# Linear-attention layer: the product of kv and wo from rounded halves, and who scales two of the queries

## The chip, the cores and the metric

The kernel runs on one core of one Trainium2 chip. The metric is the device time of one execution in microseconds (us). Three runs of the kernel before gave 863.69, 865.16 and 864.30 us, median 864.3 us.

A core has five instruction streams that run side by side: TensorE (PE, matrix products; its weight loads are listed as PEld), VectorE (DVE), ScalarE (ACT), GpSimd (POOL) and SyncE (SP), which here only starts DMA transfers. Each stream executes strictly in its program order and waits on semaphores for the others.

## The reference

Two layers, each an attention block A and an MLP block B, all in float32 on x of 2048 tokens by 448 features:

```
x = x + A(layernorm(x));  x = x + B(layernorm(x))        (twice)
A: q, k, v = split(x @ wqkv) in 16 heads of 28
   pq, pk = phi(q), phi(k),  phi(t) = (t + 1 if t > 0 else exp(t)) + 1e-6
   kv  = sum over tokens of pk^T v          (28 x 28 for each head)
   z   = sum over tokens of pk
   den = pq . z + 1e-6
   out = concat over heads(pq @ kv / den) @ wo
B: gelu(x @ w1 + b1) @ w2 + b2
```

## The kernel before

**Rounded halves.** TensorE multiplies plain float32 slowly, and a rounded format, `fp32r`, quickly. Most products are therefore made from two halves, a high half (a copy rounded to fp32r) and a low half (the original minus the high half): high times high, high times low and low times high are accumulated in one PSUM bank. A few small products are done in plain float32 instead, kv (`trans_kv`) and M (`trans_m`) among them.

**Phase 1** goes over the 16 token tiles of 128 (`phase1`, steps in `STEPS`). In each step it makes k of a tile, phi(k), its halves `kh` and `kl`, the running sum `za`, and the product G = (normalised x)^T phi(k) of the tile before. Queries phi(q) go to DRAM (`pq_d`). The last step of phase 1 in each layer is step 15.

**Between the halves of the layer** stands the passage that the change rewrites. Its order is written out by hand as a string of tokens, `ORDER`, the same for both layers; each token emits the instructions of one small function, and each engine executes its instructions in that order. The steps are: `G` (the last tile's G, with z), `gt` (G out of PSUM into four tiles), `kv` (kvp = gt^T times the v weights, 448x448 of which only the heads' blocks count), `mask` (DVE: kvm = kvp times a block mask), `m0` to `m3` (`trans_m`: M's row groups mp = kvm^T wo, 112 rows by 448 columns each, plain float32, into the four banks tagged `acc`), and `ms0` to `ms3` (`trans_ms`: Mh by ACT, Ml by DVE). With M = blockdiag(kv) @ wo the attention output is one product of scaled queries with M.

Meanwhile the first four query tiles are prepared: `qz` (POOL: pz = pq times z), `dz` (ACT: a small constant), `qd` (DVE: sum dn per head, then its reciprocal rd), `qt` (DVE: pq times rd; `qs` is `qd` and `qt` together), `tq` (PE: transpose into PSUM), `qh` (ACT: high half), `ql` (DVE: low half), and `o` (PE: twelve fp32r matmuls op, into a bank tagged `acc`). The four op banks are the same four banks that mp used: the first op, that of query 1, takes the bank of m0's result and can start only after `Ml` of that group has read it. Between these stand projections that were put off (`Q`, and `Qx`, `Qu`, `Qy` for a projection in three pieces) and `Qp`, a phi of such a projection (ACT, POOL).

After the four op blocks, five projections keep TensorE busy while the normalised rows are turned and redistributed through DRAM; then the MLP starts (hp, line 1006) and goes over blocks of 512 tokens, preparing the queries of the next block behind the matmuls.

**Tiles** of 448 columns tagged `H` hold rows of x (nine buffers in rotation), `W0` to `W6` hold the halves of the k weights in phase 1 and queries and kvm later, `S` (five buffers) stages weights, `E` and `F` (two each) hold halves. The wo rows arrive on the SP queue (`trans_load`) in two transfers after step 13.

Of the kernel before, what the change touches and what calls it, by code (L numbers as in the profile page):

```python
# [22 lines left out]
def linear_attn_mlp_kernel(  # L23
# [41 lines left out]
    NH = 9  # L65

    def t448(tag, bufs, name, dt=F32):
        bufs = NH if tag == "H" else bufs
        return work.tile([128, D], dt, name=name, tag=tag, bufs=bufs)

    APART = 28
# [7 lines left out]


    xt = {}

    def load_x(l, t):
        xt[l, t] = t448("H", 8, f"x{l}_{t}")
        sp.dma_start(xt[l, t], x_d[l][t * 128:(t + 1) * 128, :])

    load_x(0, 0)
# [550 lines left out]
    def stage_g(l, t, acc, mid=lambda: None):  # L638
# [20 lines left out]


    ORDER = [
# [3 lines left out]
    ] * LAYERS  # L665
    DEFER = NT - sum(tok in ("Q", "Qa", "Qy") for tok in ORDER[0].split())
# [15 lines left out]
    }  # L682
    NORM = (
        ((2,), (3,), (5, 6), (7, 8), (9,), (10,), (11,), (12,), (13,), (14,), (15,)),
# [42 lines left out]
    def phase1(l, tr):  # L727
        za = consts.tile([128, D], F32, name="za", tag="za")
        acc = []
        load_to(l, 4 if l == 0 else NORM[l][1][-1])  # L730
        if l == 0:
            launch(za)
            load_to(l, NORM[l][2][-1])
        for t in range(l == 0, NT):
            norm = NORM[l][t] if t < len(NORM[l]) else ()
            for tok in STEPS.get((l, t), STEP).split():
                if tok[1:].isdigit() and tok[0] in "anv":
                    {"a": stage_a, "n": stage_n, "v": stage_t}[tok[0]](l, int(tok[1:]))
                elif tok == "q1":
                    stage_qphi(1)  # L740
                elif tok == "sp":
                    for key, h in list(stored):
                        block(key)
                        spread(key, h)
                elif tok == "ld" and t + 2 < len(NORM[l]):
                    load_to(l, NORM[l][t + 2][-1])
                elif tok == "a":
                    for u in norm:
                        stage_a(l, u)
                elif tok == "n":  # L750
                    for u in norm:
                        stage_n(l, u)
                elif tok == "tu":
                    for u in norm:
                        stage_t(l, u)
                elif tok == "T" and t + 1 < NT:
                    stage_b(l, t + 1, "acc" if t == 1 else "h")
                elif tok == "X" and t + 1 < NT and (l == 0 or t + 1 >= 4):
                    stage_x(l, t + 1)
                elif tok == "K":  # L760
                    stage_k(l, t)
                elif tok == "qp":
                    stage_qphi()
                elif tok == "kp":
                    stage_kphi(l, t)
                elif tok == "kh":
                    stage_kh(l, t)
                elif tok == "kl":
                    stage_kl(l, t, za)
                elif tok == "s":  # L770
                    stage_s(l, t)
                elif tok == "G" and t >= 1:
                    acc = acc or [bank("acc", 4, f"G{c}")[:, :D] for c in range(4)]
                    stage_g(l, t - 1, acc)
                elif tok == "bg" and l == 0:
                    background(BG[t], 1 if t >= 8 else 2)
                elif tok == "Q" and t < DEFER:
                    stage_q(l, t)
            if t == 12:
                tr.wv = stage_square(wqkv[:, 2 * D:])  # L780
            if t == 13:
                trans_load(l, tr)
        return za, acc


    def trans_load(l, tr):
        tr.wo = []
        for h in range(2):
            s = half("wot")[:G, :2 * D].rearrange("p (g n) -> p g n", g=2)
            sp.dma_start(s, wo[h * 2 * G:(h + 1) * 2 * G, :].rearrange("(g p) n -> p g n", p=G))  # L790
            tr.wo += [s[:, 0], s[:, 1]]

    def trans_z(tr, za):
        zp = bank("m", 2, "zp")[:, :D]
# [8 lines left out]
    def trans_gt(tr, acc):  # L803
        tr.gt = []
        for c in range(4):
            s = t512("A" if c < 2 else "B", 2, "gt")[:, :D]
            if c < 3:
                act.copy(s, acc[c])
            else:
                dve.tensor_copy(s, acc[c])  # L810
            tr.gt.append(s)

    def trans_kv(tr):
# [6 lines left out]
    def trans_mask(tr):  # L820
# [2 lines left out]
                          tr.kvp.rearrange("p (g d) -> p g d", g=NG),  # L823
                          mask[:, None, :].to_broadcast([G, NG, G]), op=OP.mult)

    def trans_m(tr, g):
        mp = bank("acc", 4, "mp")[:G, :D]
        pe.matmul(mp, tr.kvm[:, g * G:(g + 1) * G], tr.wo[g], start=True, stop=True)  # L828
        tr.mp[g] = mp

    def trans_ms(tr, g):
        if g == 0:
# [63 lines left out]
    def q_times(l, b, j):  # L896
        pq = pqt[l, b * 4 + j]
        p3 = pq.rearrange("p (h d) -> p h d", d=DH)
        dve.scalar_tensor_tensor(p3, p3, 1e-6, rds.pop((l, b, j))[:, :, None].to_broadcast([128, H, DH]),
                                 op0=OP.add, op1=OP.mult)  # L900

    def q_scale(l, b, j, tr):
        q_den(l, b, j, tr)
# [251 lines left out]
    for l in range(LAYERS):  # L1155
# [11 lines left out]
        def pre(j):  # L1167
# [8 lines left out]
            Qx=lambda j: stage_q(l, fill[0], (0, 1)), Qu=lambda j: stage_q(l, fill[0], (2,)), Qy=lambda j: stage_q(l, fill.pop(0), (3,)),  # L1176
            Qa=lambda j: stage_q(l, fill.pop(0), tag="acc"), G=lambda j: stage_g(l, NT - 1, acc, lambda: trans_z(tr, zs[l])),
            ld=lambda j: (load_pq(l, 0, j), load_x(l, j)), gt=lambda j: trans_gt(tr, acc),
            kv=lambda j: trans_kv(tr), mask=lambda j: trans_mask(tr), m=lambda j: trans_m(tr, j),
            ms=lambda j: trans_ms(tr, j), qz=lambda j: q_z(l, 0, j, tr), qs=lambda j: q_scale(l, 0, j, tr),  # L1180
            dz=lambda j: times_tiny(pzs[l, 0, j][:, :, DH], tr.dc), dc=lambda j: times_tiny(tr.dc, tr.dc),
            qd=lambda j: q_den(l, 0, j, tr), qt=lambda j: q_times(l, 0, j),
# [75 lines left out]
```

## Time and profile before

| what | value |
|---|---|
| median of three runs | 864.3 us |
| the profiled execution: its own time, its span | 864.28 us, 862.6 us |
| PE busy | 857.9 us, 99% |
| DVE, ACT, POOL busy | 57%, 41%, 24% |
| granted TensorE clock | 1.0 throughout |
| the passage between the halves, from the end of kv to the first op | 107.03 to 112.30 us in layer 0, 531.64 to 536.90 us in layer 1 |
| the M product (mp, line 828) | 16 records for 8 products: each float32 product shows as two |

How to read it: an "x32" in a row is a count of records. Rows of the timeline give the start in us, the duration, engine, line and operands, and in brackets how long the engine idled before it and what released it. A matmul's recorded duration overlaps that of the next one, so what it costs TensorE is the distance from its start to the next start.

### The profile page before, as it was taken

To read this page: it belongs to the slowest core of one execution; us is meant where nothing else is said; L and a number is where in the kernel's file an instruction comes from. 1 tells how busy PE (TensorE), PEld (TensorE's weight loads), DVE (VectorE), ACT (ScalarE), POOL (GpSimd) and SP (SyncE) were. 2 spreads that over 40 slices of the span, in tenths; PEclk is the share of its full clock that TensorE was granted. 3 is DMA by queue.
4 is the path that set the end of the run, shared out by engine and by line. 5 is a ranking of instruction groups with operands and counts; after the bars stand their busy time and mean duration, and the time that the engine had idled before them with its cause. 6 is when DMAs were issued, how large, how long until landed. Compare 5 with 4: busy or idle time off the path is not lost.

```text
span 862.6 us, 11717 instructions
## 1 busy us (share of the span) xinstructions
PE 857.9 (99%) x4155; PEld 768.7 (89%) x4155; DVE 492.4 (57%) x962; ACT 353.0 (41%) x635; POOL 210.4 (24%) x244
## 2 busy tenths in 40 slices
PE   9999999999999999999999999999999999999998
PEld 8999988888888888888899998988888888888887
DVE  7888586559456443236477876764664383533112
ACT  7676655323323322333356565633232233233231
POOL 3576612235013012012222343120310140140000
PEclk9999999999999999999999999999999999999999
DMA  5485647633313402051145443462332423111001
GB/s 171 148 283 171 205 112 217 189 113 126 118 66 122 137 0 98 1 182 49 49 152 188 163 130 97 150 200 81 124 115 76 140 74 111 49 49 43 1 1 43
DMA packets 68681, 97.89 MB, mean 113 GB/s; under 512 B 9488, under 2 KB 62864, under 8 KB 68624
## 3 DMA queue, kind: packets, MB, share of 16 engines
q1 hardware_dynamic: 67872, 96.76, 34.8%
q8 instruction: 32, 0.52, 0.3%
q10 hardware_dynamic: 752, 0.41, 0.2%
q14 instruction: 25, 0.20, 0.1%
HBM read 57.74 MB, written 36.18 MB: 109 GB/s over the span
## 4 chain that ended last, share of the span: by engine, by line
PE 99%; DVE 0%; issue 0%; DVEq 0%
PE hp L1006 32%; PE y L1036 10%; PE y L1035 10%; PE y L1037 10%; PE G L652 8%; PE psk L366 8%; PE psq L366 7%; PE op L943 2%; PE op L942 2%; PE op L944 2%; PE op L932 1%; PE op L931 1%; PE op L933 1%; PE kvp L818 1%; PE mp L828 1%; PE psk L580 1%
## 5 line engine op out<-in xcount | busy, mean ns | idle before, releaser
L1012 DVE TENSOR_TENSOR gl<-g,gh 128x512 fp32r<-128x512 f32 x112 | 83.2, 743 | 292.8 <-ACT gh L1011 292.8
L1008 ACT ACTIVATE g<-hp,b1s 128x512 f32<-128x512 f32 x112 | 77.0, 688 | 400.9 <-PE hp L1006 400.9
L1036 PE MATMUL y<-w2l,gh 128*128 128x448 f32 x447 | 163.6, 366 | 0.0
L1035 PE MATMUL y<-w2h,gh 128*128 128x448 f32 x447 | 162.0, 362 | 0.0
L1037 PE MATMUL y<-w2h,gl 128*128 128x448 f32 x447 | 160.1, 358 | 0.0
L1006 PE MATMUL hp<-XH,w1l 128*128 128x512 f32 x336 | 130.7, 389 | 0.0
L1006 PE MATMUL hp<-XH,w1h 128*128 128x512 f32 x336 | 130.7, 389 | 0.0
L1006 PE MATMUL hp<-XL,w1h 128*128 128x512 f32 x336 | 130.1, 389 | 0.0
L216 POOL TENSOR_TENSOR brs<-bve,mhalf 128x1 f32<-128x1 f32 x55 | 34.2, 622 | 259.2 <-DVE bve L215 251.5
L1035 PEld LDWEIGHTS y<-w2h,gh 128*128 128x128 f32 x447 | 83.7, 187 | 9.4
L1036 PEld LDWEIGHTS y<-w2l,gh 128*128 128x128 f32 x447 | 83.9, 188 | 7.0
L1037 PEld LDWEIGHTS y<-w2h,gl 128*128 128x128 f32 x447 | 84.1, 188 | 4.9
L1006 PEld LDWEIGHTS hp<-XL,w1h 128*128 128x128 f32 x336 | 63.1, 188 | 13.1
L1006 PEld LDWEIGHTS hp<-XH,w1h 128*128 128x128 f32 x336 | 63.0, 188 | 10.7
L1006 PEld LDWEIGHTS hp<-XH,w1l 128*128 128x128 f32 x336 | 63.1, 188 | 9.9
L1011 ACT CAST gh<-g 128x512 fp32r<-128x512 f32 x112 | 69.6, 621 | 3.6
L366 PE MATMUL psk<-wk,XH 128*128 128x448 f32 x210 | 61.8, 364 | 0.0
L366 PE MATMUL psq<-wq,XH 128*128 128x448 f32 x196 | 57.1, 365 | 0.0
L491 POOL TENSOR_TENSOR xnl<-x,xnh 128x384 fp32r<-128x384 f32 x32 | 35.2, 1100 | 72.9 <-ACT xnh L490 59.6
L349 DVE TENSOR_TENSOR XL<-sp,XH 128x512 fp32r<-128x512 f32 x58 | 46.9, 819 | 5.7 <-ACT XH L348 5.7
L877 POOL TENSOR_TENSOR pz<-pq,zb 128x448 f32<-128x448 f32 x24 | 27.7, 1154 | 90.4 <-DVE dn L888 61.2
L652 PE MATMUL G<-kh,xnh 128*128 128x448 f32 x128 | 46.7, 367 | 0.0
(194 smaller groups left out, 1501.0 us busy)
## 6 DMA issues: line engine op xcount, KB each, us to landing
x<-in_A_x_dram SPq DMA_DIRECT2D x32, 224.0 KB, 4.2
pq_d<-eq SPq DMA_DIRECT2D x32, 224.0 KB, 2.4
pq<-pq_d SPq DMA_DIRECT2D x32, 224.0 KB, 3.4
x<-x_d SPq DMA_DIRECT2D x32, 224.0 KB, 3.7
sq_a<-sq SPq DMA_DIRECT2D x13, 512.0 KB, 2.9
sp<-sq_a SPq DMA_DIRECT2D x52, 128.0 KB, 2.9
sq_q<-sq SPq DMA_DIRECT2D x12, 512.0 KB, 2.6
sp<-sq_q SPq DMA_DIRECT2D x48, 128.0 KB, 2.8
```

What stands on the lines that cost most here:

```text
L216: pool.tensor_tensor(rs, ve, mhalf, op=OP.pow)
L349: eng.tensor_tensor(lo.rearrange("p (c i n) -> p c i n", c=4, n=32), x, f(h), op=OP.subtract)
L366: pe.matmul(o, x, p, start=(i == 0), stop=(i == 10))
L491: pool.tensor_tensor(lo[:, :TL], xn[:, :TL], f(h[:, :TL]), op=OP.subtract)
L652: pe.matmul(acc[c], w, k, start=first and c not in others[0], stop=last and c not in others[1])
L1006: pe.matmul(o, w, r, start=(k == 0), stop=(k == len(made) - 1))
L1008: act.activation(g, hp, AF.Gelu_apprx_tanh, bias=b1s[:, i:i + 1])
L1011: act.copy(gh, g)
L1012: dve.tensor_sub(gl, g, f(gh))
L1035: pe.matmul(acc[j], gh[:, s], w2h[:, i], start=first, stop=False)
L1036: pe.matmul(acc[j], gh[:, s], w2l[:, i], start=False, stop=False)
L1037: pe.matmul(acc[j], gl[:, s], w2h[:, i], start=False, stop=stop)
```

## The change

Per layer, M's product is made from halves. wo is split into `woh` (ACT, four casts of 112x448) and `wol` (two subtractions on POOL, two on DVE): three groups in step 15, the fourth after the first copy of G. wo's two transfers are issued after step 12 instead of 13. After the mask, `kvh` (ACT) and `kvl` (POOL) are the halves of kvm. Each of the four mp groups becomes three fp32r matmuls: kvh times woh, kvh times wol (`m`), and later kvl times woh (`mb`).

The mask stands ahead of query 0's denominators on DVE. Queries 2 and 3 are scaled by an addition of 1e-6 on ACT (`qa`) and a multiplication on POOL (`qg`) instead of one DVE instruction each. Query 2's transpose stands behind query 1's op block instead of ahead of it. The x tiles tagged `H` get nine names of their own, so that the halves of wo can use slots of them; the slot sequence of x is as before.

```diff
@@ x tiles
+    held = [t448(f"H{i}", 1, f"x0_{i}") for i in range(NH)]
+    slots = 0
     def load_x(l, t):
-        xt[l, t] = t448("H", 8, f"x{l}_{t}")
+        nonlocal slots
+        xt[l, t] = held[slots] if slots < NH else t448(f"H{slots % NH}", 1, f"x{l}_{t}")
+        slots += 1
@@ ORDER
-        "Q ld1 ld0 ld2 ld3 G qz1 qz0 gt dz1 dz0 qs1 qz2 dz2 Qx Qp kv qd0 qz3 dz3 dc tq1 Qu mask qt0 qh1 ql1 m0 tq0 qs2 b ms0 qh0 m1 ms1 m2 "
...
+        "Q ld1 ld0 ld2 ld3 G qz1 qz0 gt wl3 dz1 dz0 qs1 qz2 dz2 Qx Qp kv mask mh ml qd0 tq1 Qu Qy qt0 m0 qh1 ql1 qa2 qz3 dz3 dc qd2 qg2 m1 m2 mb0 mb1 tq0 m3 mb2 mb3 ms0 ms1 ms2 ms3 qh0 ql0 qa3 qd3 qg3 Qi o1 tq2 qh2 b la1 ql2 o0 tq3 qh3 Qj Qs la0 lb1 ql3 tu1 st1 o2 la2 lb0 tu0 st0 sp1 o3 la3 lb2 tu2 st2 sp0 "
@@ STEPS
+        **{(l, NT - 1): "qp K s kp w0 kh w1 kl w2 G bg" for l in range(LAYERS)},
@@ phase1
+                elif tok[0] == "w":
+                    wo_hi(tr, int(tok[1]))
+                    wo_lo(tr, int(tok[1]), pool if tok[1] in "01" else dve)
...
-            if t == 13:
+            if t == 12:
                 trans_load(l, tr)
@@ new functions
+    def wo_hi(tr, g):
+        if g == 0:
+            tr.at, tr.woh, tr.wol = slots + 4, [], []
+        tr.woh.append(t448(f"H{(tr.at + g) % NH}", 1, "woh", F32R)[:G])
+        act.copy(tr.woh[g], tr.wo[g])
+    def wo_lo(tr, g, eng):
...
+        eng.tensor_tensor(tr.wol[g], tr.wo[g], f(tr.woh[g]), op=OP.subtract)
+    def kvm_hi(tr):
+        tr.kvh, tr.kvl = (t512("E", 2, n, F32R)[:G, :D] for n in ("kvh", "kvl"))
+        act.copy(tr.kvh, tr.kvm)
+    def kvm_lo(tr):
+        pool.tensor_tensor(tr.kvl, tr.kvm, f(tr.kvh), op=OP.subtract)
     def trans_m(tr, g):
         mp = bank("acc", 4, "mp")[:G, :D]
-        pe.matmul(mp, tr.kvm[:, g * G:(g + 1) * G], tr.wo[g], start=True, stop=True)
+        s = slice(g * G, (g + 1) * G)
+        pe.matmul(mp, tr.kvh[:, s], tr.woh[g], start=True, stop=False)
+        pe.matmul(mp, tr.kvh[:, s], tr.wol[g], start=False, stop=False)
         tr.mp[g] = mp
+    def trans_m_low(tr, g):
+        mp, s = tr.mp[g], slice(g * G, (g + 1) * G)
+        pe.matmul(mp, tr.kvl[:, s], tr.woh[g], start=False, stop=True)
+    def q_add(l, b, j):
+        pq = pqt[l, b * 4 + j]
+        act.activation(pq, pq, AF.Identity, bias=tiny)
+    def q_mult(l, b, j):
+        p3 = pqt[l, b * 4 + j].rearrange("p (h d) -> p h d", d=DH)
+        pool.tensor_tensor(p3, p3, rds.pop((l, b, j))[:, :, None].to_broadcast([128, H, DH]), op=OP.mult)
```

What it does to the streams, shown for layer 0 (layer 1 is alike). Names carry buffer numbers; `pq_1`, `pq_0`, `pq_2`, `pq_3` are the four queries.

TensorE before, from the transpose of query 1, which follows kv, to the first op:

```order
L910 MATMUL tq<-ident,pq_1_1325 112x128 x4
L371 MATMUL psq<-wq_228,XH 128x448
L372 MATMUL psq<-wq_230,XH 128x448
L373 MATMUL psq<-wq_228,XL 128x448
L828 MATMUL mp<-wot,kvm 112x448
L910 MATMUL tq<-ident,pq_0_1329 112x128 x4
L828 MATMUL mp<-wot,kvm 112x448 x3
L375 MATMUL psq<-wq_265,XH 128x448
L376 MATMUL psq<-wq_265,XL 128x448
L910 MATMUL tq<-ident,pq_2_1333 112x128 x4
L931 MATMUL op<-Mh,qh 128x448
```

TensorE after, from the first mp, behind all five psq matmuls, to the first op:

```order
L859 MATMUL mp<-woh,kvh 112x448
L860 MATMUL mp<-wol,kvh 112x448
L859 MATMUL mp<-woh,kvh 112x448
L860 MATMUL mp<-wol,kvh 112x448
L859 MATMUL mp<-woh,kvh 112x448
L860 MATMUL mp<-wol,kvh 112x448
L865 MATMUL mp<-woh,kvl 112x448 x2
L954 MATMUL tq<-ident,pq_0_1341 112x128 x4
L859 MATMUL mp<-woh,kvh 112x448
L860 MATMUL mp<-wol,kvh 112x448
L865 MATMUL mp<-woh,kvl 112x448 x2
L975 MATMUL op<-Mh,qh 128x448
```

Twelve fp32r products stand where four float32 products stood; the last two psq matmuls moved ahead of them, and query 2's transpose left this stretch.

DVE before, from query 1's denominators to the low halves of M:

```order
L888 TENSOR_REDUCE dn<-pz 128x16
L892 RECIPROCAL rd<-dn 128x16
L899 SCALAR_TENSOR_TENSOR pq_1_1325<-pq_1_1325,rd 128x448
L888 TENSOR_REDUCE dn<-pz 128x16
L892 RECIPROCAL rd<-dn 128x16
L822 TENSOR_TENSOR kvm<-kvp,mask 112x448
L899 SCALAR_TENSOR_TENSOR pq_0_1329<-pq_0_1329,rd 128x448
L922 TENSOR_TENSOR ql<-tq,qh 112x512
L888 TENSOR_REDUCE dn<-pz 128x16
L892 RECIPROCAL rd<-dn 128x16
L899 SCALAR_TENSOR_TENSOR pq_2_1333<-pq_2_1333,rd 128x448
L841 TENSOR_TENSOR Ml<-mp,Mh 112x448 x4
```

DVE after, the same stretch:

```order
L812 TENSOR_TENSOR wol<-wot,woh 112x448
L924 TENSOR_REDUCE dn<-pz 128x16
L928 RECIPROCAL rd<-dn 128x16
L935 SCALAR_TENSOR_TENSOR pq_1_1337<-pq_1_1337,rd 128x448
L845 TENSOR_TENSOR kvm<-kvp,mask 112x448
L924 TENSOR_REDUCE dn<-pz 128x16
L928 RECIPROCAL rd<-dn 128x16
L935 SCALAR_TENSOR_TENSOR pq_0_1341<-pq_0_1341,rd 128x448
L966 TENSOR_TENSOR ql<-tq,qh 112x512
L924 TENSOR_REDUCE dn<-pz 128x16
L928 RECIPROCAL rd<-dn 128x16
L877 TENSOR_TENSOR Ml<-mp,Mh 112x448 x4
```

The mask moved two instructions forward, a subtraction for wo came in at the front, and query 2's scaling left.

POOL before, from the end of phase 1 to the layer norm behind the first op:

```order
L425 TENSOR_TENSOR w2l<-stg,w2h 128x448 x2
L873 TENSOR_TENSOR pz<-pq_1_1325,zb 128x16x28
L873 TENSOR_TENSOR pz<-pq_0_1329,zb 128x16x28
L873 TENSOR_TENSOR pz<-pq_2_1333,zb 128x16x28
L635 TENSOR_TENSOR eq<-ep,eq 128x448
L873 TENSOR_TENSOR pz<-pq_3_1337,zb 128x16x28
L960 TENSOR_TENSOR brs<-bst,mhalf 128x1 x4
```

POOL after, the same stretch:

```order
L812 TENSOR_TENSOR wol<-wot,woh 112x448 x2
L428 TENSOR_TENSOR w2l<-stg,w2h 128x448 x2
L909 TENSOR_TENSOR pz<-pq_1_1337,zb 128x16x28
L909 TENSOR_TENSOR pz<-pq_0_1341,zb 128x16x28
L909 TENSOR_TENSOR pz<-pq_2_1345,zb 128x16x28
L638 TENSOR_TENSOR eq<-ep,eq 128x448
L854 TENSOR_TENSOR kvl<-kvm,kvh 112x448
L909 TENSOR_TENSOR pz<-pq_3_1349,zb 128x16x28
L944 TENSOR_TENSOR pq_2_1345<-pq_2_1345,rd 128x448
L944 TENSOR_TENSOR pq_3_1349<-pq_3_1349,rd 128x448
L1004 TENSOR_TENSOR brs<-bst,mhalf 128x1 x4
```

Five instructions came in: two for wo ahead of everything, kvl between the put-off phi and query 3's pz, and the scaling of two queries ahead of the layer norm.

More of the change, by code (lines that the diff above doesn't have):

```diff
@@ L67, in t448 @@
     def t448(tag, bufs, name, dt=F32):
-        bufs = NH if tag == "H" else bufs
         return work.tile([128, D], dt, name=name, tag=tag, bufs=bufs)
@@ L791, in trans_load @@
             tr.wo += [s[:, 0], s[:, 1]]
+    def wo_hi(tr, g):
[4 more added lines that the diff above has]
+    def wo_lo(tr, g, eng):
+        if g == 3:
+            lo = t512("F", 2, "wol", F32R)[:, :D]
+        else:
+            lo = t448(("W4", "W5", f"H{(tr.at + 4) % NH}")[g], 1, "wol", F32R)
+        tr.wol.append(lo[:G])
+        eng.tensor_tensor(tr.wol[g], tr.wo[g], f(tr.woh[g]), op=OP.subtract)
     def trans_z(tr, za):
@@ L810, in trans_gt @@
                 dve.tensor_copy(s, acc[c])
+            if c == 0:
+                wo_hi(tr, 3)
             tr.gt.append(s)
@@ L1178, in linear_attn_mlp_kernel @@
             ld=lambda j: (load_pq(l, 0, j), load_x(l, j)), gt=lambda j: trans_gt(tr, acc),
+            wl=lambda j: wo_lo(tr, j, dve), mh=lambda j: kvm_hi(tr), ml=lambda j: kvm_lo(tr),
             kv=lambda j: trans_kv(tr), mask=lambda j: trans_mask(tr), m=lambda j: trans_m(tr, j),
-            ms=lambda j: trans_ms(tr, j), qz=lambda j: q_z(l, 0, j, tr), qs=lambda j: q_scale(l, 0, j, tr),
+            mb=lambda j: trans_m_low(tr, j), ms=lambda j: trans_ms(tr, j), qz=lambda j: q_z(l, 0, j, tr), qs=lambda j: q_scale(l, 0, j, tr),
             dz=lambda j: times_tiny(pzs[l, 0, j][:, :, DH], tr.dc), dc=lambda j: times_tiny(tr.dc, tr.dc),
-            qd=lambda j: q_den(l, 0, j, tr), qt=lambda j: q_times(l, 0, j),
+            qd=lambda j: q_den(l, 0, j, tr), qt=lambda j: q_times(l, 0, j), qa=lambda j: q_add(l, 0, j), qg=lambda j: q_mult(l, 0, j),
             tq=lambda j: q_transpose(l, 0, j), qh=lambda j: q_high(l, 0, j), ql=lambda j: q_low(l, 0, j), o=lambda j: o_mm(l, 0, j, tr),
```

1 row of the table ORDER is left out of this document.

## The prediction

> **What bounds the kernel now.** I read the page's shares and the chain that ended last, then what TensorE waited for, then the timeline of the passage on each engine.
>
> ```profile
> PE 857.9 (99%) x4155; PEld 768.7 (89%) x4155; DVE 492.4 (57%) x962; ACT 353.0 (41%) x635; POOL 210.4 (24%) x244
> ...
> PE 99%; DVE 0%; issue 0%; DVEq 0%
> ```
>
> ```profile
> PE warm L170 <- DVE one L164: 1.1, 1, 1.1
> ```
>
> TensorE carries the whole chain, and the third row is its only wait in the execution. So every TensorE microsecond saved is a microsecond of the end, and every new wait of it costs its full length. In layer 0 the passage reads on TensorE:
>
> ```profile
> 107.03 0.60 PE L910 MATMUL tq<-ident,pq 128*112 128x128 f32 x4
> 107.38 0.45 PE L371 MATMUL psq<-wq,XH 128*128 128x448 f32 x1
> ...
> 108.08 0.92 PE L828 MATMUL mp<-wot,kvm 112*112 112x448 f32 x2
> 108.83 0.60 PE L910 MATMUL tq<-ident,pq 128*112 128x128 f32 x4
> 109.27 2.42 PE L828 MATMUL mp<-wot,kvm 112*112 112x448 f32 x6
> ...
> 111.95 0.60 PE L910 MATMUL tq<-ident,pq 128*112 128x128 f32 x4
> 112.30 0.45 PE L931 MATMUL op<-Mh,qh 112*128 112x448 f32 x1
> ...
> 117.20 0.60 PE L910 MATMUL tq<-ident,pq 128*112 128x128 f32 x4
> ```
>
> Take distances of starts. One float32 mp costs 108.83 - 108.08 = 0.75 us, four cost 3.00. From 112.30 to 117.20 run two op blocks, 24 fp32r matmuls: 4.90/24 = 0.204 each. A transpose takes 0.35 (111.95 to 112.30), and the first matmul behind it some 0.09 more (109.27 - 108.83 = 0.44).
>
> **The products.** Twelve fp32r matmuls cost 12 x 0.204 = 2.45 us against 3.00: 0.55 us saved per layer, 1.1 in all, if TensorE never waits. That is the whole gain the change can have, 0.13% of the time. Measured against the first op: the three matmuls between 107.38 and 108.08 stay (0.70), the two moved ahead cost 0.41, so mp would start at 107.03 + 0.35 + 0.70 + 0.41 = 108.49; eight mp matmuls (1.63) end at 110.12, query 0's transpose at 110.56 with its 0.09, four more (0.82) at 111.38. Before, the first op came at 112.30 with query 2's transpose already done; without it that is 111.95, and 111.95 - 111.38 = 0.57 is the same saving seen from this side.
>
> **What the first op now waits for.** It takes the PSUM bank of the first mp and needs Ml of that group, which DVE makes. DVE in layer 0 before:
>
> ```profile
> 104.20 0.64 DVE L888 TENSOR_REDUCE dn<-pz 128x16 f32<-128x464 f32 x1 [0.65 <-ACT pz L881]
> 104.87 0.25 DVE L892 RECIPROCAL rd<-dn 128x16 f32<-128x16 f32 x1
> 105.15 1.37 DVE L899 SCALAR_TENSOR_TENSOR pq<-pq,rd 128x448 f32<-128x448 f32 x1
> 106.45 0.62 DVE L888 TENSOR_REDUCE dn<-pz 128x16 f32<-128x464 f32 x1
> 107.11 0.25 DVE L892 RECIPROCAL rd<-dn 128x16 f32<-128x16 f32 x1
> 107.28 0.58 DVE L822 TENSOR_TENSOR kvm<-kvp,mask 112x448 f32<-112x448 f32 x1
> 107.77 0.61 DVE L899 SCALAR_TENSOR_TENSOR pq<-pq,rd 128x448 f32<-128x448 f32 x1
> 108.30 0.69 DVE L922 TENSOR_TENSOR ql<-tq,qh 112x512 fp32r<-112x512 f32 x1
> ...
> 110.39 2.52 DVE L841 TENSOR_TENSOR Ml<-mp,Mh 112x448 fp32r<-112x448 f32 x4
> ```
>
> The mask hardly comes earlier: kv's last matmul is issued just ahead of 107.03, so the mask can start about 107.23 instead of 107.28. Behind it the reduction and the reciprocal now come first (0.49 + 0.66 + 0.28 from start to start), and query 0's scaling is due at 107.23 + 1.43 = 108.66. At that time POOL makes kvl: the mask ends 107.81, ACT's cast of kvm takes to 108.4, so POOL starts about 108.45. Here is what such a meeting does:
>
> ```profile
> 501.95 1.02 POOL L491 TENSOR_TENSOR xnl<-x,xnh 128x384 fp32r<-128x384 f32 x1 [2.71 <-ACT xnh L490]
> 502.92 0.77 POOL L492 TENSOR_TENSOR xnh<-x,xnh 128x64 fp32r<-128x64 f32 x1
> ```
>
> ```profile
> 502.00 1.51 DVE L349 TENSOR_TENSOR XL<-sp,XH 128x512 fp32r<-128x512 f32 x1
> ```
>
> DVE's subtraction of two SBUF operands began 0.05 us after POOL's, and ended 0.54 after POOL's end; POOL's next small one was held in turn. The scaling at 105.15 (1.37 instead of 0.61) is the same thing, against this row of POOL, which ended 106.04:
>
> ```profile
> 102.38 2.25 POOL L873 TENSOR_TENSOR pz<-pq,zb 128x448 f32<-128x448 f32 x2
> 104.91 1.13 POOL L873 TENSOR_TENSOR pz<-pq,zb 128x448 f32<-128x448 f32 x1 [0.28 <-DVE dn L888]
> 106.58 1.14 POOL L635 TENSOR_TENSOR eq<-ep,eq 128x448 f32<-128x448 f32 x1 [0.54 <-ACT eq L634]
> ```
>
> So kvl holds until 108.45 + 1.13 = 109.58, query 0's scaling ends 0.48 later (106.52 - 106.04) at 110.06, ql takes to 110.60, reduction and reciprocal to 111.55, and the first Ml runs 111.55 to 112.17. If DVE gets in first, the scaling ends at 109.28, kvl at 110.4, the first mp is complete at 110.95, Mh (0.53, row below) at 111.5, Ml at 112.15: the same. With 0.1 for the restart of TensorE the first op starts at 112.27, against the 111.38 that its own work would allow. Query 2's transpose (0.35) is still to come behind the twelve op matmuls, so layer 0 loses 112.27 + 0.35 - 112.30 = 0.32 us.
>
> ```profile
> 109.03 0.53 ACT L840 CAST Mh<-mp 112x448 fp32r<-112x448 f32 x1 [0.78 <-PE mp L828]
> ```
>
> The unknown restart lies between 0 and 0.22 (kvm ended 107.86, the first mp began 108.08, with TensorE busy between); 0.1 is near the middle.
>
> In layer 1:
>
> ```profile
> 531.89 0.57 DVE L822 TENSOR_TENSOR kvm<-kvp,mask 112x448 f32<-112x448 f32 x1
> ```
>
> ```profile
> 536.90 0.45 PE L931 MATMUL op<-Mh,qh 112*128 112x448 f32 x1
> ```
>
> With the mask at 531.85 the same steps end Ml at 536.79, the op starts at 536.89: 0.34 lost.
>
> The Trainium skill, SBUF — State Buffer, section "SBUF: two separate sides", says that GpSimd and a VectorE operation with two SBUF inputs exclude each other for a whole instruction; the 1.51 and 0.77 rows agree. By that rule the sum is a loss of 0.7 us, without it a gain of 0.7 (first rival).
>
> **wo's halves.** The casts fall into ACT's idle time of step 15 and of the copies of G:
>
> ```profile
> 97.66 0.64 ACT L530 ACTIVATE kh<-psk,tiny 128x448 fp32r<-128x448 f32 x1 [0.70 <-DVE psk L385]
> 99.04 0.57 ACT L549 CAST zh<-za 128x448 fp32r<-128x448 f32 x1 [0.74 <-DVE za L546]
> 99.51 1.03 ACT L424 CAST w2h<-stg 128x448 fp32r<-128x448 f32 x2
> 101.23 0.64 ACT L798 ACTIVATE zb<-zp,zc 128x448 f32<-128x448 f32 x1 [0.69 <-PE zp L796]
> ...
> 102.91 0.97 ACT L808 COPY gt<-G 128x448 f32<-128x448 f32 x2 [0.62 <-PE G L652]
> ```
>
> Each takes 0.57 (the zh row), in steps of about 0.5 (1.03 for two), and finds 0.70, 0.74, 0.69 and 0.62 of idle time: cost nothing. If that cover went, kh or zh would be late and G with them. wo's transfers go ahead of a w2 piece on SP; in layer 1 nothing stands between them, so the issue is as before. In layer 0:
>
> ```profile
> 88.57 0.59 SPq L128 DMA_DIRECT2D stg<-in_A_wqkv_dram  x1
> ...
> 93.06 0.88 SPq L790 DMA_DIRECT2D wot<-in_A_wo_dram  x2
> ```
>
> ```profile
> wot<-in_A_wo_dram SPq DMA_DIRECT2D x2, 392.0 KB, 5.4
> ```
>
> Issued at 93.06 and 5.4 us under way, wo would miss the first cast (due at 97.66 - 0.70 = 96.96); issued right behind the row of 88.57 it lands around 95. Cost nothing.
>
> The second of POOL's two subtractions follows a cast that ends about 98.8 and takes 1.13, to about 100. In layer 0 POOL's w2l pair and both pz then come 0.5 to 0.9 us later, since the w2h casts moved by a step of ACT and the port is shared; DVE's fourth subtraction (after G's copy, 103.5) meets a pz, which moves the first dn from 104.20 to about 104.8, the phi on ACT and POOL (106.58) with it, and kvl behind that by up to 0.3. The bounds are 0 and 0.3; I take 0.1 for layer 0.
>
> **Queries 2 and 3.** Their additions follow qh on ACT. Query 2's multiplication on POOL waits for the reciprocal of 111.55 and ends 1.13 later, 112.7; query 3's waits for the one behind four Ml (2.52), ql (0.60), 0.66 and 0.28, 115.6, and ends 116.8. Their transposes are due 114.7 and 117.5: hidden by the op blocks. DVE loses 0.6 per query, which is what lets Ml start where it does; the layer norm of query 1's rows comes 0.6 later on DVE, hidden because the fourth one ends the stage. That stage has room:
>
> ```profile
> 132.89 1.28 DVE L349 TENSOR_TENSOR XL<-sp,XH 128x512 fp32r<-128x512 f32 x2
> ```
>
> ```profile
> 133.74 4.99 PE hp L1006 x22
> ```
>
> The last XL ends 134.17. In the first hp seven of the eleven matmuls (4.99/22 = 0.227 each) stand ahead of those that read low halves, so XL is wanted at 135.33: about 1.1 us of slack, and both sides move together.
>
> **Sum.** 0.32 + 0.34 + 0.1 = 0.76 us lost. The profiled execution took 864.28 us (span 862.6), and the median is 864.3, so both give 865.1 us.
>
> **Rivals.**
>
> First, faster: DVE and POOL don't hold each other there. Then query 0's scaling ends at 109.28, DVE is free at 110.8, the first Mh, from an mp complete at 110.2, ends 110.8, Ml 111.45, the op starts 111.55, and layers gain 0.40 and 0.36: 863.5 us. It decides if Ml ends before 111.85. For it: query 0's scaling at 107.77 took only 0.61 beside a POOL instruction. Against it: the 1.37 and 1.51 rows. The limit of this side, no wait at all, is 864.28 - 1.1 = 863.2.
>
> Second, clearly slower: the port is not yielded between the two pz rows, so the fourth wo subtraction on DVE waits for both. In layer 0 it then ends near 106.0, the first dn near 106.6, query 1's scaling (behind the third pz) at 108.2, and the mask, which stands behind that, starts at 108.2 instead of 107.23: 1.0 more, 866.1, and up to 866.6 if ACT's casts come late too. For it: both pz run back to back (2.25). Against: in the 501.95 rows DVE got in between two POOL instructions. It decides once dn starts later than about 105.4.
>
> **Chances.** Forecast, a loss of 0.2 to 1.7 us: 0.57. First rival, from a gain of 1.2 to a loss of 0.2: 0.21. Second, a loss above 1.7: 0.17. Left over, faster by more than the products can give: 0.05. The range runs from 863.3 to 866.5. A difference of 0.2%, 1.7 us, is about what a measurement of this kernel can tell from none: faster by more 0.05, within 0.78, slower by more 0.17.
>
> **What would show it.** Right: mp as 24 short records; TensorE with a wait of 0.7 to 0.9 us at the first op, released by DVE's Ml; query 0's scaling on DVE at 1.2 to 1.4 us beside kvl; dn at 104.8. Wrong: no TensorE wait there, or waits at the first mp (kvh late), at mb (kvl later than 110.5), or in G of step 15 (kh or zh late behind a cast, or wo not landed).

## The result, and the profile after

The changed kernel takes 866.34 us (median of 12 runs, 865.65 to 868.44), the kernel before in the same comparison 864.51 us (863.69 to 865.93): a ratio of 1.0023, with an interval of 1.0014 to 1.0031. It is slower, by about 1.8 us. A second set of 11 runs of the same program (below, "changed again") gave a ratio of 1.0013 [1.0004, 1.0022], with the medians 1.4 us apart. The forecast was 0.8 us slower.

The profiled execution took 865.65 us with a span of 863.7 us, against 864.28 and 862.6. TensorE's waits after (engine, line, what it waited for: us in total, times, longest; left out is the wait of 1.1 us at the very start, which the kernel before has too):

```profile
...
PE op L975 <- DVE Ml L877: 0.8, 2, 0.4
PE tp L275 <- DVE x L1189: 0.4, 1, 0.4
PE psk L583 <- ACT wk L140: 0.3, 1, 0.3
PE G L655 <- DVE kl L542: 0.2, 1, 0.2
```

The first row is the forecast wait, once in each layer. The next two lie in the first 50 us, and what TensorE waits for there differs from profile to profile (the repeat of before has one of the two, the first profile of before neither). The last lies near the start of layer 1, at 448 us, and no step of the prediction had it.

The passage in layer 0 on TensorE, after (start, duration, line, operands, idle time before and its releaser):

```profile
103.58 3.31 PE L841 MATMUL kvp<-gt,stg 128*112 128x112 f32 x32
...
108.20 0.46 PE L859 MATMUL mp<-woh,kvh 112*112 112x448 f32 x1
108.50 0.36 PE L860 MATMUL mp<-wol,kvh 112*112 112x448 f32 x1
...
109.52 0.66 PE L865 MATMUL mp<-woh,kvl 112*112 112x448 f32 x2
110.09 0.62 PE L954 MATMUL tq<-ident,pq 128*112 128x128 f32 x4
110.47 0.45 PE L859 MATMUL mp<-woh,kvh 112*112 112x448 f32 x1
...
110.97 0.56 PE L865 MATMUL mp<-woh,kvl 112*112 112x448 f32 x2
111.95 0.47 PE L975 MATMUL op<-Mh,qh 112*128 112x448 f32 x1 [0.43 <-DVE Ml L877]
112.26 0.36 PE L976 MATMUL op<-Ml,qh 112*128 112x448 f32 x1
```

The same time on VectorE and on GpSimd:

```profile
106.92 0.62 DVE L845 TENSOR_TENSOR kvm<-kvp,mask 112x448 f32<-112x448 f32 x1 [1.01 <-PE kvp L841]
107.47 0.62 DVE L924 TENSOR_REDUCE dn<-pz 128x16 f32<-128x464 f32 x1
108.12 0.25 DVE L928 RECIPROCAL rd<-dn 128x16 f32<-128x16 f32 x1
108.41 1.58 DVE L935 SCALAR_TENSOR_TENSOR pq<-pq,rd 128x448 f32<-128x448 f32 x1
109.92 0.68 DVE L966 TENSOR_TENSOR ql<-tq,qh 112x512 fp32r<-112x512 f32 x1
110.52 0.62 DVE L924 TENSOR_REDUCE dn<-pz 128x16 f32<-128x464 f32 x1
111.17 0.25 DVE L928 RECIPROCAL rd<-dn 128x16 f32<-128x16 f32 x1
111.34 2.15 DVE L877 TENSOR_TENSOR Ml<-mp,Mh 112x448 fp32r<-112x448 f32 x4
```

```profile
108.29 1.16 POOL L854 TENSOR_TENSOR kvl<-kvm,kvh 112x448 fp32r<-112x448 f32 x1 [0.27 <-ACT kvh L851]
109.41 1.59 POOL L909 TENSOR_TENSOR pz<-pq,zb 128x448 f32<-128x448 f32 x1
111.57 0.94 POOL L944 TENSOR_TENSOR pq<-pq,rd 128x448 f32<-128x448 f32 x1 [0.56 <-DVE rd L928]
```

Query 0's scaling starts 0.12 us behind kvl and ends 0.54 us after kvl does. The first op waits for the first of the four Ml, and these start only after that scaling, query 1's low half and query 2's denominators.

To compare kernels, I cut TensorE's timeline at five starts: kv's product, the first op, the first hp of the other half, and the first and the third G of layer 1 (the stretch between these two is called the seam of the layers here, 440.79 to 454.15 us before; some of the expectations below give its ends other names, but mean these two). The stretches not shown are equal within 0.02 us in all profiles but for one, named below. With float32 M the record of the first op overlaps the product ahead of it, so "kv to op" reads some 0.3 short where the op doesn't wait. All in us:

| kernel | kv starts, layer 0 | kv to op, layers 0, 1 | kv to hp, layers 0, 1 | seam | sum against before | median against before |
|---|---|---|---|---|---|---|
| before | 103.88 | 8.42, 8.41 | 29.70, 29.69 | 13.36 | | |
| before, again | 104.09 | 8.42, 8.40 | 29.70, 29.68 | 13.31 | -0.1 | +0.2 |
| changed | 103.58 | 8.37, 8.37 | 30.18, 30.21 | 13.82 | +1.5 | +1.8 |
| changed, again | 103.79 | 8.38, 8.37 | 30.18, 30.15 | 13.75 | +1.3 | +1.4 |
| query 2's denominators first | 104.61 | 7.80, 7.77 | 29.47, 29.49 | 13.53 | -0.3 | +0.5 |
| queries 2, 3 on VectorE | 103.96 | 9.10, 9.10 | 30.90, 30.90 | 13.64 | +2.7 | +3.1 |
| query 0's denominators ahead of the mask | 103.83 | 7.75, 8.06 | 29.51, 29.89 | 13.57 | +0.2 | +0.4 |
| M in float32 | 103.79 | 8.17, 8.17 | 29.93, 29.93 | 13.20 | +0.3 | +1.0 |
| M in float32, query 0 ahead | 103.99 | 7.70, 7.69 | 29.69, 29.69 | 13.20 | -0.2 | +0.1 |
| seam's buffers as before | 105.14 | 8.37, 8.37 | 30.17, 30.18 | 13.36 | +1.0 | +0.3 |
| both repairs | 103.71 | 7.79, 7.78 | 29.49, 29.47 | 13.68 | -0.1 | -0.6 |
| query 0 ahead, seam's buffers | 103.61 | 7.77, 8.08 | 29.54, 29.85 | 13.63 | +0.3 | +0.9 |
| before, nine names | 103.98 | 8.42, 8.41 | 29.70, 29.68 | 13.25 | -0.1 | -0.4 |
| three products in layer 1 only | 103.63 | 7.70, 7.78 | 29.69, 29.48 | 13.20 | -0.4 | +0.4 |

"Sum" is the two passages (kv to hp) and the seam less those of before; "median" is each kernel's median less that of the kernel before in the same comparison. Before's first op has query 2's transpose (0.35 us) already behind it, the others' has not (only the kernel before, its repeat and the one with nine names have it there). Two things are left out of the sum: when kv starts in layer 0, which differs by up to 1.6 us between profiles of nearly equal programs, and what an execution loses where its profile wasn't taken. So sum and median agree to no better than about 0.7 us. They do agree that the changed kernel and the one with queries 2 and 3 on VectorE stand apart, and that the others lie within a microsecond of before.

For the changed kernel: 0.48 and 0.52 us are lost in the passages and 0.46 at the seam, and this profile's kv started 0.30 earlier. That makes 1.16, which is the difference of the spans (1.1).

### The profile page after: what moved, and what is told of

Its sections match the earlier page's. It is cut to its first block, busy times and chain, and to the rows that moved or that the text cites. A ratio compares the mean times of both kernels' runs of the same rounds, so it can differ in the third digit from the quotient of the medians.

```text
span 863.7 us, 11774 instructions
## 1 busy us (share of the span) xinstructions
PE 857.3 (99%) x4163; PEld 768.6 (89%) x4163; DVE 494.6 (57%) x962; ACT 359.3 (42%) x649; POOL 222.1 (26%) x254
## 4 chain that ended last, share of the span: by engine, by line
PE 96%; DVE 2%; DMA 1%; issue 0%; ACT 0%; POOL 0%; DVEq 0%; POOLq 0%; SPq 0%
PE hp L1050 32%; PE y L1080 10%; PE y L1079 10%; PE y L1081 10%; PE G L655 8%; PE psk L369 7%; PE psq L369 7%; PE op L987 2%; PE op L986 2%; PE op L988 2%; PE op L975 1%; PE op L976 1%; PE op L977 1%; PE kvp L841 1%; PE op L990 1%; PE op L989 1%
```

## The experiments

Each comparison ran in five rounds beside the kernel before.

**Repeats.** The kernel before, unchanged:

> The kernel before once more, against itself. It shows how far two profiles of one program differ at the launch (first 15 us) and at the seam of the layers (434 to 455 us), where the changed kernel's profile started 0.3 us earlier and lost 0.46 us. If these are chance, the ratio's interval holds 1 and this profile's seam differs from the first profile by some tenths too; if the loss at the seam belongs to the change, both profiles of this kernel agree there within 0.1 us.

Measured: ratio 0.9999 [0.999, 1.0008], stretches as before within 0.05 us. The changed kernel, unchanged:

> The changed kernel once more, to see what a second profile of it gives for the same stretches and to have it on the chip of the three kernels beside it. Theory: the wait at the first op again (0.35 to 0.45 us in each layer), passages 30.1 to 30.3 us, seam 13.5 to 13.9 us, the time 1.6 to 2.2 us above the kernel before. If the passages or the seam of the first profile were chance, they move by more than 0.15 us here.

Measured: 866.26 us, ratio 1.0013 [1.0004, 1.0022], the same wait, passages 30.18 and 30.15, seam 13.75. The passages repeat to 0.06 us and are no chance; the seam is 0.4 us above before's again.

**What the first op waits for.** Query 2's denominators on VectorE stand ahead of query 0's scaling, so that kvl is done when the scaling starts:

```diff
-"... ml qd0 tq1 Qu Qy qt0 m0 qh1 ql1 qa2 qz3 dz3 dc qd2 qg2 m1 ..."
+"... ml qd0 tq1 Qu Qy qd2 qt0 m0 qh1 ql1 qa2 qz3 dz3 dc qg2 m1 ..."
```

> Edit: the changed kernel, with query 2's reduction and reciprocal ahead of query 0's scaling on DVE. Theory (the first op waits for Ml, because DVE's scaling of query 0 stands still until POOL's kvl gives the port back, with two DVE instructions behind it): the two instructions fill the 0.9 us of standing still, the scaling takes 0.6 instead of 1.58 us, TensorE's wait at the first op (0.4 us by the wait rows, 0.57 by the distance of starts) is gone in both layers; 0.8 to 1.1 us less than the changed kernel, within 0.2% of the kernel before. Rival (TensorE's own new matmuls and their weight loads make the passage longer): the wait moves to another instruction, the time stays within 0.2 us of the changed kernel.

VectorE and GpSimd in this kernel (its kv starts 1.03 us later than the changed kernel's):

```profile
110.39 0.64 DVE L935 SCALAR_TENSOR_TENSOR pq<-pq,rd 128x448 f32<-128x448 f32 x1
```

```profile
109.33 1.16 POOL L854 TENSOR_TENSOR kvl<-kvm,kvh 112x448 fp32r<-112x448 f32 x1 [0.27 <-ACT kvh L851]
110.45 1.59 POOL L909 TENSOR_TENSOR pz<-pq,zb 128x448 f32<-128x448 f32 x1
```

The scaling takes 0.64 instead of 1.58 us, and the wait at the first op is gone in both layers: kv to op 7.80 and 7.77 instead of 8.37, passages 0.71 and 0.72 us shorter than the changed kernel's. The time was 865.11 us, ratio 1.0006 [0.9997, 1.0015]. So the wait came from the meeting of the scaling and kvl, as forecast.

The opposite: queries 2 and 3 scaled by one VectorE instruction each again, in the changed order.

```diff
-qa2 ... qd2 qg2 ... qa3 qd3 qg3
+... qs2 ... qs3
```

> Edit: the changed kernel with queries 2 and 3 scaled by one DVE instruction each, as before; all else as changed. Theory (DVE's list up to Ml sets the first op): one instruction of 0.6 us more ahead of Ml makes TensorE's wait at the first op 0.55 us longer in each layer, 1.1 us more than the changed kernel. Rival (the wait comes from elsewhere, the first mp or Mh): no difference from the changed kernel.

Its waits on TensorE:

```profile
PE op L975 <- DVE Ml L877: 2.3, 2, 1.1
```

Kv to op grew by 0.73 and the passages by 0.72 and 0.69 us, where 0.55 was expected. The four Ml start 8.42 us after kv instead of 7.76, so the 0.6 us of the scaling on VectorE stand on the path in full. 867.74 us, ratio 1.0035 [1.0023, 1.0046]. In this order VectorE is what the first op waits for, and work moved from it pays.

One part undone: query 0's denominators ahead of the mask again.

```diff
-"... Qx Qp kv mask mh ml qd0 tq1 ..."
+"... Qx Qp kv qd0 mask mh ml tq1 ..."
```

> The changed kernel with query 0's reduction and reciprocal on VectorE back ahead of the mask; there VectorE stands idle 1.0 us for the end of kv's product. Nothing else is changed. Theory (the loss of the passage is query 0's scaling standing behind kvl on GpSimd, and everything behind it): the scaling follows the mask at once, before kvl begins; it meets only the end of GpSimd's phi and takes 0.6 to 1.1 us instead of 1.58; no TensorE wait at the first op; from kv's product to the first op 7.6 to 7.85 us instead of 8.37, passages 0.2 to 0.4 us shorter than the 29.70 before, the time 1.4 to 1.9 us under the changed kernel's. Rival (the loss is the four Ml after all, 2.15 us on VectorE, or ScalarE's pairs of Mh): the wait at the first op stays at 0.3 us or more though VectorE is free earlier.

In layer 0 it came out as the theory has it: scaling 1.04 us, no wait at the op, kv to op 7.75. In layer 1 not quite (VectorE):

```profile
530.15 1.38 DVE L935 SCALAR_TENSOR_TENSOR pq<-pq,rd 128x448 f32<-128x448 f32 x1
531.45 0.62 DVE L924 TENSOR_REDUCE dn<-pz 128x16 f32<-128x464 f32 x1
532.11 0.25 DVE L928 RECIPROCAL rd<-dn 128x16 f32<-128x16 f32 x1
532.28 0.56 DVE L845 TENSOR_TENSOR kvm<-kvp,mask 112x448 f32<-112x448 f32 x1
```

There query 1's scaling meets a pz on GpSimd (529.91 to 531.05), the denominators follow it at 531.45, and the mask starts 0.67 us after kv's last matmul was issued; TensorE waits 0.25 at the first mp for kvh, and kv to op is 8.06. So the mask ahead of the denominators is right in layer 1 and gains nothing in layer 0. 864.75 us, ratio 1.0006 [0.9997, 1.0015]: a loss of 0.35 us where the changed kernel lost 1.4 and 1.8.

**What three products save.** M in float32, all else as changed; halves of kv and wo are not made (the main edit; their tokens and casts go too):

```diff
-pe.matmul(mp, tr.kvh[:, s], tr.woh[g], start=True, stop=False)
-pe.matmul(mp, tr.kvh[:, s], tr.wol[g], start=False, stop=False)
+pe.matmul(mp, tr.kvm[:, s], tr.wo[g], start=True, stop=True)
```

> Edit: the changed kernel with M's product in four float32 matmuls again, without the halves of wo and kvm; mask, queries 2 and 3 and the transpose stay as changed. Theory (DVE's list up to Ml sets the first op): the scaling of query 0 now meets query 3's pz on POOL instead of kvl, TensorE still waits about 0.3 us at the first op, and the time is within 0.3 us of the changed kernel. Rival (the halves and their extra work on ACT and POOL are the loss): the loss goes, the time is that of the kernel before.

The passage was 0.25 and 0.28 us shorter than the changed kernel's, not the same, and no wait at the op is named; the time was 865.62 us, ratio 1.0005 [0.9996, 1.0014]. With kvl gone, GpSimd's pz for query 3 takes its place, and the scaling still meets it (VectorE, then GpSimd):

```profile
108.62 1.37 DVE L931 SCALAR_TENSOR_TENSOR pq<-pq,rd 128x448 f32<-128x448 f32 x1
```

```profile
108.38 1.14 POOL L905 TENSOR_TENSOR pz<-pq,zb 128x448 f32<-128x448 f32 x1 [0.75 <-DVE dn L920]
```

Its Ml start 7.56 us after kv (111.35 - 103.79), those of the changed kernel 7.76, so the float32 matmuls, which end later, just about cover them. This run couldn't price the products, since VectorE still ended last or nearly so. The next one could: the same with query 0's denominators ahead of the mask.

```diff
-"... Qx Qp kv mask qd0 tq1 ..."
+"... Qx Qp kv qd0 mask tq1 ..."
```

> The kernel with query 0 ahead of the mask, and M by one float32 product as before, without halves of kv and wo. Neither has a wait at the first op, so the difference to the kernel with three products is the products themselves. If they save what the prediction summed: 0.55 us per layer. From the rows of the runs so far (the first of the short matmuls 0.10 longer, the restart behind the pair with kvl): 0.40 us per layer, so from kv's product to the first op 8.0 to 8.1 us, passages 29.65 to 29.8, the time 0.8 us above the kernel with three products.

No wait, passages 29.69 in both layers, 864.47 us, ratio 1.0003 [0.9994, 1.0012]. Here is its TensorE around the scaled products (a record of the first op overlaps the product ahead of it, so I read the second):

```profile
103.99 3.31 PE L838 MATMUL kvp<-gt,stg 128*112 128x112 f32 x32
...
108.59 2.42 PE L856 MATMUL mp<-wot,kvm 112*112 112x448 f32 x6
110.84 0.60 PE L950 MATMUL tq<-ident,pq 128*112 128x128 f32 x4
111.28 0.92 PE L856 MATMUL mp<-wot,kvm 112*112 112x448 f32 x2
...
112.24 0.37 PE L972 MATMUL op<-Ml,qh 112*128 112x448 f32 x1
```

and that of the kernel with three products and no wait at the op (query 2's denominators first):

```profile
104.61 3.31 PE L841 MATMUL kvp<-gt,stg 128*112 128x112 f32 x32
...
109.24 0.46 PE L859 MATMUL mp<-woh,kvh 112*112 112x448 f32 x1
109.54 0.36 PE L860 MATMUL mp<-wol,kvh 112*112 112x448 f32 x1
...
110.55 0.65 PE L865 MATMUL mp<-woh,kvl 112*112 112x448 f32 x2
111.13 0.62 PE L954 MATMUL tq<-ident,pq 128*112 128x128 f32 x4
...
112.61 0.36 PE L976 MATMUL op<-Ml,qh 112*128 112x448 f32 x1
```

The second op starts 112.24 - 103.99 = 8.25 us after kv with float32, 112.61 - 104.61 = 8.00 with three products: 0.25 us saved per layer, and 0.21 over the whole passage (29.69 against 29.48). These two differ in VectorE's order as well. In the same order, with query 0's denominators ahead of the mask, layer 0 gives 8.05 us to the second op and a passage of 29.51 with three products, so 0.20 and 0.18 saved. The rest of the change without the products (scaling on ScalarE and GpSimd, order of TensorE, names), in this order, moves nothing: 29.69 against 29.70.

**The seam.** In the changed kernel x1_5 (tile 5 of layer 1's x) takes the buffer of x_12 (tile 12 of the rows stored ahead of it), whose store must land first; before, that of x1_0. Undone:

```diff
-t448(f"H{slots % NH}", 1, f"x{l}_{t}")
+t448(f"H{ {37: 5, 38: 1, 39: 2, 40: 3, 41: 4}.get(slots, slots % NH)}", 1, f"x{l}_{t}")
```

> The changed kernel with one thing undone: at the seam of the layers x1_5 takes the buffer of x1_0 and x1_6 to x1_9 those of x_12 to x_15, as before the change; nine names are kept, all else is as changed. Theory (the new names let x1_5 inherit the buffer of x_12, whose store must land first, and that is what the changed kernel loses between the layers): SyncE's wait of x<-x_d on x_d<-x between 433 and 443 us is gone, the stretch from the last G of step 14 to the second G of layer 1's step 1 (13.36 us before, 13.82 in the changed kernel) is back at 13.2 to 13.45, the passages stay 0.4 to 0.6 us longer than before each, and the time is 0.3 to 0.6 us below the changed kernel's. Rival (the seam varies from run to run by itself; the same program gave 13.36 and 13.31): the stretch stays at 13.5 to 13.9 with or without the wait, and the time is the changed kernel's within 0.2 us.

The seam was 13.36, the time 865.11, 1.15 us under the changed kernel beside it. SyncE's wait for a store did not go, it moved to the load behind x1_5's (0.6 us). Still, this looked like the cause. Both repairs together:

> The two repairs together: the buffers at the seam as before, and query 2's reduction and reciprocal ahead of query 0's scaling on VectorE. If the wait at the first op and the seam are the two causes and add up: passages 0.2 to 0.25 us shorter than before in each layer, seam as before, so 0.3 to 0.5 us faster than the kernel before (ratio 0.9994 to 0.9996, too small to be told from none), and 2.0 us under the changed kernel. If something else in the change costs time outside the passages and the seam: the time stays 0.3 us or more above the kernel before although the two stretches are repaired.

864.27 us, ratio 1.0 [0.9989, 1.001], but with a seam of 13.68. And the names alone, put into the kernel before:

> The kernel before with nothing but the nine named x buffers in turn. Theory: passages as before (8.42 and 29.70 us) in both layers, the wait of x<-x_d on x_d<-x appears on SyncE between 433 and 443 us, the seam takes 13.5 to 13.9 us instead of 13.3, and the time is 0.2 to 0.6 us above the kernel before. Rival (the names alone cost nothing; it is the later end of the passage that makes the stores and the loads meet): no difference from the kernel before within 0.2 us, seam 13.3 to 13.4.

The wait of a load on a store appears on SyncE (1.0 us, at the load behind x1_5's), yet the seam is 13.25 and the time 864.48, ratio 0.9994 [0.9986, 1.0003]. Names without a loss, old buffers with one: the theory falls, as the whole cause at least. So does the pair with query 0 ahead of the mask:

> The same, and at the seam of the layers the buffers as before the change. If the naming costs at the seam in most executions: 0.3 to 0.6 us under the kernel with query 0 ahead of the mask alone, and 0.6 to 0.9 us under the kernel before. If the seam is chance whatever the naming (a lateness of x1_5 that goes with the issue of the four stores before it): the same time as that kernel within 0.3 us.

865.26 us, ratio 1.0005 [0.9996, 1.0014], with a seam of 13.63; the kernel beside it without the edit took 864.75 with 13.57. (This profile also lost 1.02 us between the seam and layer 1's kv.)

What separates the seams in the table is another thing: all eight kernels with three products in layer 0 have 13.36 to 13.82 us (mean 13.62), the five with float32 there 13.20 to 13.36 (mean 13.26). So the last run has float32 in layer 0 and three products in layer 1 (one of its edits):

```diff
-**{(l, NT - 1): "qp K s kp w0 kh w1 kl w2 G bg" for l in range(LAYERS)},
+**{(l, NT - 1): "qp K s kp w0 kh w1 kl w2 G bg" for l in range(1, LAYERS)},
```

> M by one float32 product in layer 0 (with query 0's reduction and reciprocal ahead of the mask) and by three products of halves in layer 1 (with query 2's reduction ahead of query 0's scaling); the rest as changed. Known from earlier runs: passage 29.7 us in layer 0, 29.5 in layer 1, no wait at the first op, 0.2 us under the kernel before in sum. Open is the stretch between the layers: 13.2 to 13.36 us in five profiles of kernels with float32 M, 13.36 to 13.82 in eight with three products, where in each one of the four stores of x ahead of x1_5's load took some 2 us to issue. If what layer 0 issues makes the difference: 13.2 to 13.36 here, the four stores in 1.9 us together, the time 0.1 to 0.3 us under the kernel before. If it is chance, or goes with the program as a whole: 13.5 to 13.8, the stores 3 us or more, the time 0.1 to 0.3 above.

The seam was 13.20 and the passages as known. So in these profiles the seam's loss goes with the halves in layer 0. That is a pattern over 14 profiles, nearly all of different kernels, and the two groups touch at 13.36. What is late is the arrival of x1_5. Where VectorE starts on it, before:

```profile
440.49 0.63 DVE L210 BATCH_NORM_STATS2 bst<-x 128x6 f32<-128x448 f32 x1 [0.24 <-DMA x<-x_d]
```

after:

```profile
441.12 0.63 DVE L213 BATCH_NORM_STATS2 bst<-x 128x6 f32<-128x448 f32 x1 [0.70 <-DMA x<-x_d]
```

and in the last run, with no wait:

```profile
439.92 0.62 DVE L213 BATCH_NORM_STATS2 bst<-x 128x6 f32<-128x448 f32 x1
```

The load stands on SyncE behind four stores of x. Their issue before and after:

```profile
434.22 1.92 SPq L1042 DMA_DIRECT2D x_d<-x  x4
436.24 2.04 SPq L85 DMA_DIRECT2D x<-x_d  x2
```

```profile
434.40 3.55 SPq L1086 DMA_DIRECT2D x_d<-x  x4
438.57 0.81 SPq L88 DMA_DIRECT2D x<-x_d  x2
```

and the issues of the four one by one (shortest, median and longest in ns), after:

```profile
L1086 SPq DMA_DIRECT2D x_d<-x x4: 338/381/2008, 434.4 to 437.5; - x4
```

One of the four took 2.01 us to issue, where the others took 0.34 to 0.42. All kernels with three products in layer 0 had a long one here, of 1.3 to 2.0 us (2.9 to 3.6 us for the four). The load is issued later for it. Where the new names come with three products in layer 0, it then waits another 0.5 to 1.1 us for x_12's store to land; so the names do add to the lateness there, though what that costs is not shown (seams of 13.53 to 13.82 in these five kernels, 13.36 to 13.68 in the three with the old buffers). In the eight kernels the load is issued 2.4 to 3.4 us ahead of layer 1's first G, in the six others 3.0 to 4.6. The long store isn't the whole cause: the four took 3.5 us in the repeat of before and 3.1 in the last run, and they lost nothing or next to nothing. Why the halves of layer 0, over 300 us earlier, make x1_5 late stays open. The last run doesn't settle the time either: 864.92 us, ratio 1.0008 [0.9997, 1.0018]. Its profile has the shortest span of all (861.9 us), eight of its runs have spans up to 862.8 and four of 863.5 to 865.3, and what those four lost no profile shows.

## Why the prediction was right, and where its sizes were off

- **TensorE carries the end.** Right. What the passages gain or lose, the span shows.
- **When mp starts.** Forecast 108.49 with kv at 103.88, so 4.61 us after kv; measured 4.62. The mask starts 3.34 us after kv, as forecast (3.35).
- **The products.** The direction was right, the term was mis-sized: the prediction gave 0.55 us per layer from twelve matmuls of 0.204, and 0.18 to 0.25 was measured. The first eight took 1.89 us (109.24 to 111.13 in the kernel without a wait at the op), not 1.63. The first matmul takes 0.30, 0.10 more than the rest. The pair with kvl takes 0.58, 0.17 more than the second such pair (0.41): query 0's transpose, which comes behind it, starts 0.10 after the scaling of query 0 ends (111.03). Only part of this is a wait for VectorE, which the view of waits doesn't name. With query 0's denominators ahead of the mask the scaling ends at 108.76, long before the transpose, and the pair still takes 0.50:

```profile
109.83 0.66 PE L865 MATMUL mp<-woh,kvl 112*112 112x448 f32 x2
110.33 0.60 PE L954 MATMUL tq<-ident,pq 128*112 128x128 f32 x4
```

So some 0.09 belongs to the first product with kvl, and some 0.08 to the scaling. The prediction had counted on every matmul of the row at 0.204 and on a transpose that is always ready.
- **The wait at the first op.** The mechanism was right in all parts: kvl, scaling, query 2's denominators, Ml. Forecast: op 8.39 us after kv in layer 0 and 8.40 in layer 1; measured 8.37 in both. Forecast wait 0.7 to 0.9; measured 0.43 and 0.41 by the rows, 0.57 and 0.60 against the kernel without it. The wait is shorter because TensorE's own work came 0.3 later (7.80 us after kv where it doesn't wait, forecast 7.50). The four Ml started 7.76 us after kv, forecast 7.67. Where two chains meet, the error on the shorter one didn't move the end: the good hit on the op's start says nothing for the price of the products.
- **The port.** Query 0's scaling was forecast at 1.2 to 1.4 us and took 1.58. The Trainium skill, SBUF — State Buffer, section "SBUF: two separate sides", says that GpSimd and a VectorE operation with two SBUF inputs share a pair of SBUF ports, and that whichever of the two begins first holds the pair for its whole instruction. The trace agrees for both sides: VectorE held 1.58 and 1.37 us behind GpSimd, GpSimd held 1.59 us (instead of 1.14) behind a scaling of 0.64. The first rival, without this, is out. Its one piece of evidence, a scaling that took only 0.61 beside GpSimd in the kernel before, was read from VectorE's side alone; there it was GpSimd that stood still, for a pz that takes 1.14 elsewhere:

```profile
107.68 1.70 POOL L873 TENSOR_TENSOR pz<-pq,zb 128x448 f32<-128x448 f32 x1
```

Its record starts 0.09 us ahead of the scaling's (107.77), so records this close don't tell who was first. The second rival, with VectorE's wo subtraction behind both pz in layer 0, is out too. These are that subtraction and the reduction behind it on VectorE, and the pz on GpSimd:

```profile
103.09 1.33 DVE L812 TENSOR_TENSOR wol<-wot,woh 112x448 fp32r<-112x448 f32 x1
104.34 0.62 DVE L924 TENSOR_REDUCE dn<-pz 128x16 f32<-128x464 f32 x1
```

```profile
102.79 4.13 POOL L909 TENSOR_TENSOR pz<-pq,zb 128x448 f32<-128x448 f32 x3
```

In layer 0 the subtraction got in between two pz that stood back to back. The reduction came 0.76 us after kv's start (before 0.32, forecast 0.9). The lateness of kvl for which 0.1 us was set aside in layer 0 wasn't its consequence: kvl started 4.71 us after kv in both layers (forecast 4.57, without the 0.1).
- **Behind the first op.** Here a term was missing. The prediction added only query 2's transpose (0.35) behind the op. From op to hp the changed kernel takes 21.81 us, before 21.28: 0.18 more than the transpose explains. 0.11 of it is the start after a wait: the first op takes 0.31 to the next instead of 0.20. For 0.07 I have no row. So the passages lost 0.48 and 0.52 us instead of 0.42 and 0.34.
- **wo's halves.** Right: ScalarE's casts filled idle time. Ahead of zb ScalarE idled 0.69 before and idles 0.23 now, with the chain to G unmoved:

```profile
100.93 0.64 ACT L819 ACTIVATE zb<-zp,zc 128x448 f32<-128x448 f32 x1 [0.23 <-PE zp L817]
```

- **Queries 2 and 3.** Right that GpSimd's scaling is hidden (query 2's ends 112.51, its transpose is at 114.48), and that VectorE's 0.6 us per query is what this buys: 0.7 us of the passage in the run that puts them back.
- **What the sum left out.** The seam: 0.46 us in this profile, 0.36 in the mean of eight kernels against five. The description of the change said that the slot sequence of x is as before. That was wrong: from x1_5 on, other buffers are taken. But that alone cost nothing in the kernel before, and the loss came with the halves. The forecast of 0.76 us became 1.0 in the passages and about 0.4 at the seam, which is the 1.4 us of the second comparison; of the 1.8 us of the first, 0.4 are in no profile. The forecast reached up to a loss of 1.7: the second comparison lies inside, the first just above, where the second rival stood, whose condition (dn later than about 105.4) did not come true. So the mechanism was right and the size too small, mostly for want of a term at the seam.

The version with both repairs saves 0.43 us in the passages and gave 864.27 us: no difference from the kernel before that can be measured, and the best that this change came to.

## What to carry to other kernels

Before replacing a product by cheaper ones, ask what the engine would then wait for: here 0.18 to 0.25 us per layer was to be had, and a 1.16 us subtraction on GpSimd, put where VectorE wants two SBUF operands, cost 0.57. Such a meeting is cured by order alone, by placing on VectorE at that time an instruction that GpSimd doesn't hold up (here query 2's reduction, 0.64 us beside kvl). And the price of a short matmul in a long row doesn't hold at the joints, at the start after a wait or a change of kind, where each cost 0.1 us more here.

## What the runs showed of the hardware

- A multiplication on GpSimd with one operand spread over 28 columns (128x448) takes 0.94 us, one with two full operands 1.13 to 1.16 where nothing holds it up.
- SyncE issues a store of 224 KB in 0.32 to 0.42 us, but single ones in 1.3 to 2.0, and not in every profile of the same program: four in 1.92 in one profile of the kernel before, in 3.50 in the other.
- A kernel's span varies by 1 to 3.4 us from run to run at a granted clock of 0.997 to 1.0: 861.9 to 865.3 us for the last one.
